# Loading the first q and k group ahead of the first W3 quarter, with new load and clock numbers in the build-time planner

## The chip, the cores and the metric

The kernel runs on one core of one Trainium2 chip. The metric is device microseconds of one execution; lower is better. The span of a profile is about 2 us shorter than the measured time of the same execution.

## The reference, cut to what matters

```python
q_n = q / (norm(q) + 1e-6);  k_n = k / (norm(k) + 1e-6)     # q, k, v: (8, 12, 448, 64)
attn = softmax(q_n @ k_n.T / tau)                            # tau = 0.1
x = (attn @ v), heads put side by side                       # (3584, 768)
a = x @ w1;  b = x @ w2                                      # 768 x 1024 each
return ((a * b) @ w3) @ w_out                                # 1024 x 1024, 1024 x 768
```

## The kernel before

The kernel multiplies W3 by W_out once, on TensorE, so that the last two products become one. It walks over 48 pairs of heads (8 batches of 6 pairs; three pairs are one load group) and fills TensorE's free time with W3 transposes, W3 x W_out products and projections. All of this is cut into small steps, and **a planner in Python decides at build time in which order each engine gets its steps**. It keeps a modelled clock for each engine and each load, and takes the step that can start first; among those within a small tolerance it takes the lowest rank. On the chip every engine runs its list in that order and waits wherever data is late. For each pair the steps are: square, sum, root and scale (they normalise q and k), a transpose on TensorE with its copy, scores, exponential, attention-times-V. The *spread* copies a loaded v group into the tile that attention-times-V reads.

```python
class Plan:
    HOP = 0.25                        # us from one engine to another
    RATE = 0.4e3                      # KB per us of the load queue
    DMA_FIRST, DMA_LAST = 1.2, 1.2
    ...
    def order(self):
        ...
        ready = {n for n, k in left.items() if k == 0}       # a set of strings
        self.lanes, ring = [], 0.0
        while ready:
            found = {}
            for n in ready:
                for eng, cost in steps[n]["on"]:
                    t = self.earliest(n, eng)
                    if t is not None:
                        found.setdefault(eng, []).append((t, n, cost))
            ...
            tmin, eng = min((min(f)[0], e) for e, f in found.items())
            tol = 0.15 if eng == "PE" else 0.05
            t, n, cost = min((f for f in found[eng] if f[0] <= tmin + tol),
                             key=lambda f: (steps[f[1]]["rank"], f[0]))
            ...
            if st["kb"]:
                ring = max(ring, t + cost + self.DMA_FIRST) + st["kb"] / self.RATE
                self.end[n], self.where[n] = ring + self.DMA_LAST, "DMA"
```

The first pair (pair 0) comes in float32 by two fast queues; all else is loaded and cast by GpSimd's queue, in this order, with at most 8 loads in flight:

```python
loads = ["w30", "q0", "k0", "wo0", "v0", "w31", "q1", "k1", "w32", "w33", "v1", "wo1", "q2",
         "k2", "w10", "v2", "w20"]        # w30: first quarter of W3; wo0: first half of W_out
...
for n in range(60):                       # warm-up on zeros: two matmuls a group, only where
    add(f"warm{n}", [("PE", 0.4)], 10000 + n, lambda e: warm(),     # nothing else can run
        takes=[("pm", ("warm", n))], later=f"warm{n - 1}" if n else None, until=11.0)
```

Of the kernel before, what the change touches and what calls it, by code (L numbers as in the profile page):

```python
# [19 lines left out]
class Plan:  # L20
# [6 lines left out]

    HOP = 0.25
    LANES = 8
    RATE = 0.4e3  # L30
    DMA_FIRST, DMA_LAST = 1.2, 1.2

    def __init__(self, rings, begin):
        self.rings, self.free = rings, dict(begin)
# [8 lines left out]
    def add(self, name, on, rank, emit, after=(), takes=(), holds=(), kb=0, later=None,  # L43
            until=None, slack=0.0, port=False):
        self.steps[name] = dict(on=on, rank=rank, emit=emit, after=list(after), later=later,
                                takes=list(takes), kb=kb, until=until, slack=slack, port=port)
        for key in holds:
            self.holders.setdefault(key, []).append(name)
# [30 lines left out]
    def order(self):  # L79
        steps = self.steps  # L80
        needs = {n: [a for a in st["after"] + [st["later"]] if a and a not in self.end]
                 for n, st in steps.items()}
        users = {}
        for n, need in needs.items():
            for a in need:
                users.setdefault(a, []).append(n)
        left = {n: len(need) for n, need in needs.items()}
        ready = {n for n, k in left.items() if k == 0}
        self.lanes, ring = [], 0.0
        self.port = dict(DVE=0.0, POOL=0.0)  # L90
        out = []
        while ready:
# [6 lines that stand above are left out]
            if not found:  # L99
                break  # L100
# [4 lines that stand above are left out]
            st = steps[n]  # L105
            out.append((t, len(out), n, eng))
            ready.discard(n)
            self.start[n], self.free[eng] = t, t + cost
            self.end[n], self.where[n] = t + cost, eng
            if st["port"] and eng in self.port:  # L110
                self.port[eng] = t + cost
# [3 lines that stand above are left out]
                self.lanes.append(self.end[n])  # L115
            for r, key in st["takes"]:
                self.taken[r].append(key)
            for u in users.get(n, ()):
                left[u] -= 1
                if left[u] == 0:  # L120
                    ready.add(u)
        late = [n for n, st in steps.items() if n not in self.end and st["until"] is None]
        assert not late, late[:10]
        return [(n, e) for _, _, n, e in sorted(out)]
# [3 lines left out]
def kernel(  # L128
# [12 lines left out]
    nc = tc.nc  # L141
# [282 lines left out]
    ident = const.tile([128, 128], BF16)  # L424

    def warm():
        ps = psM.tile([128, 512], FP32, tag="pm", name="ps_warm")
        for _ in range(2):
            nc.tensor.matmul(ps[:, :S], warm_sb[:, :128], warm_sb[:, :S], start=True, stop=True)

    def ones():
        for t in v_tiles:
            nc.gpsimd.memset(t[:, :, :, D:D + 1], 1.0)
# [5 lines left out]
        begin=dict(PE=1.0, ACT=3.0, DVE=1.2, POOL=1.3))  # L439
    add = plan.add  # L440

    add("ident", [("POOL", 0.6)], -90, lambda e: make_identity(nc, ident), later="wo0")
    add("ones", [("POOL", 0.45)], -70, lambda e: ones())
    every = slice(None)
    w3_part = [slice(k, k + 2) for k in range(0, KO2, 2)]
# [1 line left out]
                   wo0=(wo_sb, moe_w_out, every, slice(0, NH)),  # L447
                   wo1=(wo_sb, moe_w_out, every, slice(NH, DM)))
    for n, part in enumerate(w3_part):
        weights[f"w3{n}"] = (w3_sb, moe_w3, part, every)  # L450
    loads = ["w30", "q0", "k0", "wo0", "v0", "w31", "q1", "k1", "w32", "w33", "v1", "wo1", "q2",
             "k2", "w10", "v2", "w20"]
    for g in range(3, NG):
        loads += [f"q{g}", f"k{g}", f"v{g}"]
    before = None
# [157 lines left out]
                     [] if mh else [("out_sb", ("out_sb", bb, ch))], [("big", bb)],  # L613
                     holds2=[("out_sb", bb, ch)] if mh else [])
    for n in range(60):
        add(f"warm{n}", [("PE", 0.4)], 10000 + n, lambda e: warm(),
            takes=[("pm", ("warm", n))], later=f"warm{n - 1}" if n else None, until=11.0)

    for n, e in plan.order():
# [37 lines left out]
```

## Time and profile before

| | before |
|---|---|
| time, median of the first 3 runs | 406.42 us (406.42 to 406.82) |
| span of the profile | 404.3 us |
| TensorE busy | 395.0 us |
| warm-up matmuls (two in a group) | 40, 10.9 us |
| first W_out product starts | 16.50 us |
| last matmul ends | 400.17 us |

TensorE is busy almost everywhere, so the busy share says little.

### The profile page before, as it was taken

The numbers are of one execution on the slowest core, as the hardware profiler recorded it, in microseconds if no ns is written. First come the engines' busy times: TensorE is split into PE (matmuls) and PEld (weight loads), VectorE is DVE, ScalarE is ACT, GpSimd is POOL, SyncE is SP. The second block draws the span as 40 slices with busy tenths as digits, with TensorE's granted clock in tenths as the row PEclk, the third lists the DMA queues.
The fourth block names the chain that finished last, engine by engine and source line by source line (L and its number), as shares of the span: only waits on it lengthen the run. The fifth ranks groups of instructions, "written<-read, shape, count | busy, mean of one in ns | idle before, by whom it ended". The sixth has DMA issues, their size and how long they took to land.

```text
span 404.3 us, 9387 instructions
## 1 busy us (share of the span) xinstructions
PE 395.0 (98%) x3944; PEld 234.9 (58%) x3944; DVE 216.3 (53%) x484; ACT 247.9 (61%) x399; POOL 245.9 (61%) x258
## 2 busy tenths in 40 slices
PE   8799999999999999999999999999999999999995
PEld 3466665556555666555655566556655566555553
DVE  2785647587576755766655766444344443420310
ACT  3687777766676676757776757566656676323222
POOL 7479899999999999999999999315100000000000
PEclk9899999999999999999999999999999999999999
DMA  8999999256585285753745365000210013103005
GB/s 144 201 206 207 210 199 153 36 70 104 119 102 71 36 153 113 101 68 36 141 82 70 38 106 123 30 2 2 79 39 2 2 41 84 36 0 105 14 5 153
DMA packets 42474, 35.18 MB, mean 87 GB/s; under 512 B 1856, under 2 KB 36416, under 8 KB 42432
## 3 DMA queue, kind: packets, MB, share of 16 engines
q0 software_dynamic: 37312, 23.11, 41.0%
q1 hardware_dynamic: 4752, 11.07, 9.4%
q8 instruction: 31, 0.51, 0.5%
q10 hardware_dynamic: 368, 0.40, 0.3%
q14 instruction: 11, 0.09, 0.1%
HBM read 46.66 MB, written 11.01 MB: 143 GB/s over the span
## 4 chain that ended last, share of the span: by engine, by line
PE 73%; POOL 19%; DMA 3%; issue 2%; DVE 1%; ACT 0%; POOLq 0%; DVEq 0%
PE ps_b L336 15%; PE ps_a L336 14%; PE ps_o L336 14%; PE ps_av L301 10%; PE sc L284 9%; POOL sq L229 8%; POOL nrm L255 7%; PE ps_w L336 5%; PE ps_tr L268 4%; DMA wo_sb<-in_moe_w_out_dram 3%; PE ps_tb L323 2%; POOL raw L198 2%; POOL v_sb L214 2%; PE ps_w L349 1%; POOL w_sb L217 0%
## 5 line engine op out<-in xcount | busy, mean ns | idle before, releaser
L292 ACT ACTIVATE expT<-sc 112x896 bf16<-112x896 f32 x192 | 166.0, 916 | 43.2 <-PE sc L284 42.9
L336 PEld LDWEIGHTS <-w_sb 128*128 128x128 bf16 x768 | 69.6, 98 | 57.2 <-issue 4.1
L255 POOL TENSOR_TENSOR nrm<-raw,rn 112x512 bf16<-112x512 bf16 x90 | 90.8, 1036 | 2.2 <-PE ps_tr L268 2.1
L229 POOL TENSOR_TENSOR sq<-raw 112x512 bf16<-112x512 bf16 x87 | 87.8, 1037 | 0.2
L336 PE MATMUL ps_b<-xT,w_sb 128*128 128x448 bf16 x384 | 83.2, 353 | 0.0
L336 PE MATMUL ps_a<-xT,w_sb 128*128 128x448 bf16 x384 | 83.0, 352 | 0.0
L336 PE MATMUL ps_o<-w_sb,abT 128*128 128x384 bf16 x448 | 80.1, 326 | 0.0
L235 DVE TENSOR_REDUCE ss<-sq 112x8 f32<-112x512 bf16 x96 | 64.0, 679 | 15.2 <-POOL sq L229 14.9
L382 DVE TENSOR_TENSOR abT<-a_sb,ps_b 128x448 bf16<-128x448 bf16 x64 | 39.6, 619 | 57.7 <-PE ps_b L336 54.8
L301 PEld LDWEIGHTS <-expT 112*128 112x128 bf16 x1536 | 59.2, 98 | 19.4 <-issue 8.8
L371 ACT CAST a_sb<-ps_a 128x448 bf16<-128x448 f32 x64 | 34.0, 532 | 52.4 <-PE ps_a L336 51.5
L301 PE MATMUL ps_av<-v_sb,expT 112*128 112x65 bf16 x1536 | 65.2, 194 | 0.0
L284 PE MATMUL sc<-qkT 64*112 64x448 bf16 x384 | 56.9, 374 | 1.4 <-DVE qkT L276 1.3
L336 PEld LDWEIGHTS <-abT 128*128 128x128 bf16 x448 | 41.3, 98 | 26.5 <-issue 2.7
L342 ACT COPY out_sb<-ps_o 128x384 f32<-128x384 f32 x43 | 20.6, 478 | 38.0 <-PE ps_o L336 36.5
L314 DVE TENSOR_TENSOR osd<-ps_av,rs 128x256 bf16<-128x256 f32 x96 | 40.7, 424 | 3.3
L313 DVE RECIPROCAL rs<-ps_av 128x4 f32<-128x4 f32 x96 | 17.1, 178 | 46.2 <-PE ps_av L301 45.9
L214 POOL COPY v_sb<-vraw 112x1536 bf16<-112x1536 bf16 x16 | 23.4, 1460 | 24.4 <-PE ps_av L301 24.0
L276 DVE COPY qkT<-ps_tr 128x896 bf16<-128x896 bf16 x48 | 29.7, 619 | 12.1 <-PE ps_tr L268 12.1
L330 DVE COPY xT<-ps_tb 128x448 bf16<-128x448 bf16 x48 | 18.6, 387 | 20.5 <-PE ps_tb L323 20.2
L284 PEld LDWEIGHTS <-qkT 64*112 64x112 bf16 x384 | 17.3, 125 | 20.7 <-issue 16.4
L268 PEld LDWEIGHTS <-nrm 112*128 112x128 bf16 x384 | 21.9, 99 | 12.1 <-issue 6.6
(37 smaller groups left out, 220.3 us busy)
## 6 DMA issues: line engine op xcount, KB each, us to landing
vraw<-in_v_dram POOLq DMA_DIRECT2D x16, 336.0 KB, 4.8
raw<-in_q_dram POOLq DMA_DIRECT2D x15, 336.0 KB, 5.6
raw<-in_k_dram POOLq DMA_DIRECT2D x15, 336.0 KB, 7.6
w_sb<-in_moe_w_dram POOLq DMA_DIRECT2D x2, 1536.0 KB, 25.4
out_dram<-out_sb SPq DMA_DIRECT2D x7, 336.0 KB, 2.8
out_dram<-out_sb SPq DMA_DIRECT2D x8, 288.0 KB, 3.0
w_sb<-in_moe_w_dram POOLq DMA_DIRECT2D x4, 512.0 KB, 16.2
out_dram<-out_sb SPq DMA_DIRECT2D x8, 240.0 KB, 2.8
```

The lines of the kernel that those rows point to most:

```text
L214: nc.gpsimd.tensor_copy(v_tiles[g % NV][:, :, :, :D], vraws.pop(g))
L229: eng.tensor_mul(o, x, x)
L235: nc.vector.reduce_sum(sss[g][:, t, 2 * i:2 * i + 2, :], sqs.pop((g, i, t)), axis=AX.X)
L255: eng.tensor_mul(nrms[g][:, i, t].rearrange("p j h d -> p h j d"), raw_of(g, t, i), rns[g][:, t, 2 * i:2 * i + 2].to_broadcast([P, 2, NJ, D]))
L268: nc.tensor.transpose(ps[:, t, j * P:(j + 1) * P], n[:, i, t, j].rearrange("p h d -> p (h d)"), ident[:P, :P])
L284: nc.tensor.matmul(sc[:P, hh, :S], qks[pp][64 * hh:64 * hh + 64, 1, c * P:(c + 1) * P], qks[pp][64 * hh:64 * hh + 64, 0, :], start=True, s ...
L292: nc.scalar.activation(exps[pp][:, c], scs.pop((pp, c))[:P, :, :S], ACT.Exp, scale=1.0 / float(tau))
L301: nc.tensor.matmul(ps[:, m, :], exps[pp][:, c, hh, q0:q0 + 128], vt[:, 2 * i + hh, c, :], start=(c == 0), stop=(c == NJ - 1))
L314: nc.vector.tensor_mul(osds[pp][:, :, hh, :], ps[:, :, :D], rs.to_broadcast([128, NJ, D]))
L336: nc.tensor.matmul(o, l, r, start=(i == 0), stop=(i == len(pairs) - 1))
L371: nc.scalar.copy(a_sbs[b, fo], pms.pop(("a", b, fo))[:, :S])
L382: nc.vector.tensor_mul(abts[b // 2][:, fo, c0:c0 + S], a_sbs.pop((b, fo)), pms.pop(("b", b, fo))[:, :S])
```

## The change

The intent: the first q and k group land sooner so that attention can start, and the planner is told what the load queue and the cold TensorE clock really take, so that its order fits. The diff is complete.

```diff
--- before.py
+++ after.py
@@ -27,8 +27,9 @@
 
     HOP = 0.25
     LANES = 8
-    RATE = 0.4e3
-    DMA_FIRST, DMA_LAST = 1.2, 1.2
+    RATE = 0.385e3
+    RING_FREE = 3.8
+    DMA_FIRST, DMA_LAST = 1.2, 1.5
 
     def __init__(self, rings, begin):
         self.rings, self.free = rings, dict(begin)
@@ -86,7 +87,7 @@
                 users.setdefault(a, []).append(n)
         left = {n: len(need) for n, need in needs.items()}
         ready = {n for n, k in left.items() if k == 0}
-        self.lanes, ring = [], 0.0
+        self.lanes, ring = [], self.RING_FREE
         self.port = dict(DVE=0.0, POOL=0.0)
         out = []
         while ready:
@@ -439,7 +440,7 @@
         begin=dict(PE=1.0, ACT=3.0, DVE=1.2, POOL=1.3))
     add = plan.add
 
-    add("ident", [("POOL", 0.6)], -90, lambda e: make_identity(nc, ident), later="wo0")
+    add("ident", [("POOL", 0.6)], -90, lambda e: make_identity(nc, ident), later="w30")
     add("ones", [("POOL", 0.45)], -70, lambda e: ones())
     every = slice(None)
     w3_part = [slice(k, k + 2) for k in range(0, KO2, 2)]
@@ -448,8 +449,8 @@
                    wo1=(wo_sb, moe_w_out, every, slice(NH, DM)))
     for n, part in enumerate(w3_part):
         weights[f"w3{n}"] = (w3_sb, moe_w3, part, every)
-    loads = ["w30", "q0", "k0", "wo0", "v0", "w31", "q1", "k1", "w32", "w33", "v1", "wo1", "q2",
-             "k2", "w10", "v2", "w20"]
+    loads = ["q0", "k0", "w30", "wo0", "v0", "w31", "q1", "k1", "w32",
+             "w33", "v1", "wo1", "q2", "k2", "w10", "v2", "w20"]
     for g in range(3, NG):
         loads += [f"q{g}", f"k{g}", f"v{g}"]
     before = None
@@ -613,7 +614,7 @@
                      [] if mh else [("out_sb", ("out_sb", bb, ch))], [("big", bb)],
                      holds2=[("out_sb", bb, ch)] if mh else [])
     for n in range(60):
-        add(f"warm{n}", [("PE", 0.4)], 10000 + n, lambda e: warm(),
+        add(f"warm{n}", [("PE", 0.78 if n < 4 else 0.39)], 10000 + n, lambda e: warm(),
             takes=[("pm", ("warm", n))], later=f"warm{n - 1}" if n else None, until=11.0)
 
     for n, e in plan.order():
```

## The prediction

> **What bounds the kernel now.** I read the page first, then the chain of waits in order of time, then the timeline of the first 30 us, then windows of 1 us over the first 24 us. The page says where time can be lost at all:
>
> ```profile
> PE 395.0 (98%) x3944; PEld 234.9 (58%) x3944; DVE 216.3 (53%) x484; ACT 247.9 (61%) x399; POOL 245.9 (61%) x258
> ```
>
> TensorE is idle for 404.3 - 395.0 = 9.3 us of the span. The timeline places it: 1.26 us before the first warm-up matmul, 404.3 - 400.17 = 4.1 us after the last matmul (last copy and store), some 2.6 us between 11 and 17 us, and about 1.2 us in all the rest (windows: 0.78 us lost between 100 and 177 us, 0.37 between 177 and 300, nothing after). So from 16.5 us on TensorE is a queue of work, and the end is 16.5 + that work + 4.1. The other engines have slack (61% at most); the long stretch of GpSimd in the chain from 95 to 177 us ends in a TensorE wait of only 0.37 us. A change of load order can pay only in what TensorE does before that queue starts, in its clock there, and in new holes. Busy there isn't useful: 32 + 8 matmuls of the head are warm-up on zeros, 10.9 us.
>
> ```profile
> 3.58 12.87 DMA wo_sb<-in_moe_w_out_dram
> 16.50 2.02 PE ps_w L336 x8
> ```
>
> The chain of waits: the first half of W_out is issued at 3.58 us and lands 12.9 us later; from its landing the chain is TensorE. Its wait itself is short (0.73 us). What had TensorE done by then that is useful?
>
> ```profile
> 4.45 0.63 ACT L227 ACTIVATE sq<-raw 112x512 bf16<-112x512 f32 x1 [1.96 <-DMA raw<-in_k_dram]
> 10.17 1.06 PE L349 MATMUL ps_w<-ident,w_sb 128*128 128x128 bf16 x16
> 10.82 1.29 DVE L344 COPY w3t_sb<-ps_w 128x1024 bf16<-128x1024 bf16 x2 [3.32 <-PE ps_w L349]
> 11.28 0.63 ACT L227 ACTIVATE sq<-raw 112x512 bf16<-112x512 bf16 x1 [3.50 <-DMA raw<-in_q_dram]
> 12.02 0.68 DVE L235 TENSOR_REDUCE ss<-sq 112x8 f32<-112x512 bf16 x1
> 12.62 0.68 DVE L255 TENSOR_TENSOR nrm<-raw,rn 112x512 bf16<-112x512 f32 x1
> 13.29 0.56 PE L268 MATMUL ps_tr<-ident,nrm 112*128 112x112 bf16 x8
> 15.19 0.59 PE L284 MATMUL sc<-qkT 64*112 64x448 bf16 x4 [1.34 <-DVE qkT L276]
> 16.81 0.90 ACT L292 ACTIVATE expT<-sc 112x896 bf16<-112x896 f32 x1
> ```
>
> The key reading is the sixth line. Pair 0 comes by its own fast queues at 4.2 to 4.5 us, and ScalarE has its last root (rn, 7.57 + 0.21 us) at 7.8. Its second scale could run then; it runs at 12.62, because VectorE takes its instructions in program order and the planner put before it the two W3 copies (10.82, W3 landed about 9.5) and the sum of a square that waits for the q group (landed 11.3). The planner had thought these loads earlier: with its numbers (0.4 MB/us, ring free at 0, 1.2 + 1.2 us) W3 lands at 3.3 + 2.62 + 1.2 = 7.1, q0 at 8.3, W_out at 13.3. Landed: 9.5, 11.3, 16.5. Useful TensorE work before 16.5 us is thus two W3 transposes, one pair transpose, half the scores of pair 0, at warm durations about 1.06 + 0.45 + 0.55 = 2.1 us. The holes have a price too:
>
> ```profile
> 14.00:15.00 1.00, 0.00 (x0) 0.00 (x0) 1.00 (x3) 0.94 (x4) 0.15 (x2) 1.00 1.43 201
> 17.00:18.00 1.00, 1.00 (x6) 0.53 (x5) 1.00 (x2) 0.71 (x1) 0.62 (x1) 0.65 1.21 199
> 18.00:19.00 1.00, 1.00 (x10) 0.83 (x8) 0.23 (x1) 0.46 (x2) 0.47 (x1) 0.50 1.37 202
> 19.00:20.00 1.00, 0.91 (x7) 0.38 (x5) 0.62 (x1) 1.00 (x3) 1.00 (x2) 0.50 1.38 197
> 20.00:21.00 1.00, 1.00 (x11) 0.61 (x11) 0.00 (x0) 1.00 (x2) 0.79 (x2) 0.64 1.44 199
> ```
>
> The last three columns are granted clock, DMA share, GB/s. TensorE stands still at 14 to 15 us and is then given half its clock: missing clock 0.35 + 0.50 + 0.50 + 0.36 = 1.7 us.
>
> **What the Trainium skill says.** "TensorE: Matmul & The Clock Gate", Part 1, says the clock is half speed by default, that about 3.4 us of sustained work releases it, and that an idle window of the same free-running length takes it back. The trace agrees in kind: the warm-up's weight loads come every 0.37 us up to 7.1 and every 0.19 us after, and the slow spell above lasts from 17.35 to about 20.7 = 3.4 us. "DMA: Bandwidth & Descriptors", Anatomy of one DMA, puts a load through GpSimd at about 2.0 us plus bytes over 436 GB/s. Steady flow agrees: W_out (1.57 MB read) lands 16.5 - 12.7 = 3.8 us after k0, 0.41 MB/us. The first 10 us don't: they move 138 to 172 GB/s of written bf16 a microsecond, against about 200 later.
>
> **The change, part by part.** No arithmetic is added or removed; all instructions keep their costs. Three things move.
>
> (1) q0 and k0 (0.46 MB read each) go ahead of the first W3 quarter (1.05 MB). Landings are my estimate: the same bytes through the same queue. From about 4.4 us at the measured 0.15 MB/us written: q0 is 0.23 MB written, 1.5 us, and about 1.3 us to completion: 7.3; k0 8.8; W3 comes last of the three and takes k0's old place, 12.3 to 12.7. The sum of the three is unchanged, so W_out stays at 16.5, v0 18.5, the second W3 quarter about 20.9, q1 22.5, k1 24.7, the third quarter 27.0. Gain for q0 and k0 about 4 us, loss for W3 about 3.
>
> (2) The planner's new numbers, worked by hand: q0 3.8 + 1.19 + 1.5 = 6.5, k0 7.7, W3 10.4, W_out 14.5, v0 16.3, second quarter 19.0, third 25.3. Against my real landings they are still early by about 2 us, no longer by 3. Pair 0's second scale is planned at about 8.4 and the W3 copies only after 11, so the scale goes ahead of them.
>
> (3) Warm-up: four groups at 0.78, the rest at 0.39. The planner fills TensorE to about 9.5 with some 18 groups in place of 16. In the trace 8 groups are slow (16 matmuls in 5.9 us), so it is still too many: 1.26 + 8 x 0.735 + 10 x 0.375 = 10.9 us. That, and no longer the data, should gate pair 0's transposes.
>
> Then, with the durations above: transposes at 10.9 (13.29 before); copy to 12.1; the W3 transposes, planned ahead of the first scores, at 12.5 when W3 has landed; first scores about 13.0 (15.19 before); first exponential about 13.2 (16.81). By W_out's landing TensorE can have done both W3 transposes, two pair transposes, all scores of pair 0: 1.06 + 2 x 0.45 + 2 x 0.55 = 3.1 us, 1.0 more than before. If TensorE then isn't idle long enough to lose its clock, another 1.5 us: 2.5 us. Against that stands v0: it still lands at 18.5, and its spread (1.48 us on GpSimd) gives 20.1 at best, 20.8 as traced before. Before, the first attention-times-V came at 22.7, late enough; now TensorE will have W_out products (2 x 1.3), the scores of pair 1 and a transpose, all done near 20.0, and wait some 0.8 us. Net 2.5 - 0.8 = 1.7 us. A second count agrees: the work done by 22.54 before (a third W3 transpose instead of a second half of scores, both about 0.5 us) is done by 20.85. After that TensorE is a queue again and the lead should last to the end: 406.42 - 1.7 = 404.7.
>
> **Rivals.** (a) The head stays bound by loads: W_out, v0 and the weight quarters keep their times, and TensorE meets each as late as before, above all the third quarter at 27.0, where it waited 0.43 us already. For it: the before order tracks the planner at a constant lag of 3 us there (13.55 planned, 16.5 run; 23.95 and 27.0). Against it: q1 and k1 leave plenty of attention work in reserve at that time. It would make 406. (b) GpSimd becomes the bound: it is over 90% busy from 30 to 250 us, and its stream starts with q1, which doesn't come sooner. For it: the chain goes through it for 80 us. Against it: TensorE lost only 0.78 us in that stretch, as the projections fill whatever attention leaves. It would eat the whole gain: 406.4. (c) Everything fits: the clock stays up, no wait for v0, the two stray holes vanish: 406.42 - 4 = 402.4. (d) The new order, fixed at build time, meets new holes of 0.5 to 1 us, or the slow clock comes one window later because W3 is late: 407.5. One more spread: ties of the planner are settled by the order of a set of strings, which needn't be the same in two builds, so a few tenths either way are order luck.
>
> **Range and chances.** The middle is 404.7; (a) and (b) pull up by 1.7, (c) down by 2.3. I give 402.2 to 407.0 eight in ten. Two per cent is 8.1 us; the whole head has only 2.6 us of idle time, 1.7 of lost clock and 10.9 of warm-up that mostly waits for data, so faster by 2% is nearly ruled out, as is slower.
>
> **What would show it.** Right: pair 0's transposes at about 11 us after more warm-up matmuls (36 or so in a row), first q-group square near 7.5, W3 transposes near 12.5, W_out products still at 16.5, no window of half clock between 17 and 21, first attention-times-V near 21, a last matmul 1.7 us sooner. Wrong: W_out's landing moved by over 1 us, half clock again, or TensorE busy time from 30 us on lower by over 1 us.

## The result

In the same rounds the changed kernel took 405.87 us (median of 4 runs, 404.98 to 406.30) and the kernel before 406.42. Ratios here are the mean time of one kernel's runs over that of the other's of the same rounds, so not quite the ratio of the medians. It is 0.9983, with a 95% interval of 0.9964 to 1.0003. In microseconds that is -0.7 (+0.1 to -1.5). The forecast of -1.7 lies outside.

TensorE's row of the page of the changed kernel, to be held against 395.0:

```profile
PE 392.7 (97%) x3944; PEld 233.5 (58%) x3944; DVE 217.9 (54%) x487; ACT 246.0 (61%) x396; POOL 245.9 (61%) x258
```

TensorE is busy 2.3 us less, but the span is only 0.4 us shorter: more of it is now idle. The timeline of the changed kernel (start, length, engine, line, what; in brackets the idle time before and what ended it) answers to the one of before:

```profile
7.09 0.63 ACT L228 ACTIVATE sq<-raw 112x512 bf16<-112x512 bf16 x1 [0.33 <-DMA raw<-in_q_dram]
8.75 0.69 DVE L256 TENSOR_TENSOR nrm<-raw,rn 112x512 bf16<-112x512 f32 x1 [0.32 <-ACT rn L251]
10.03 0.56 PE L269 MATMUL ps_tr<-ident,nrm 112*128 112x112 bf16 x8
10.81 1.06 PE L350 MATMUL ps_w<-ident,w_sb 128*128 128x128 bf16 x16
11.80 0.58 PE L285 MATMUL sc<-qkT 64*112 64x448 bf16 x4
12.82 1.73 ACT L293 ACTIVATE expT<-sc 112x896 bf16<-112x896 f32 x2
13.40 0.37 PE L269 MATMUL ps_tr<-ident,nrm 112*128 112x112 bf16 x4 [1.01 <-DVE nrm L256]
14.95 1.46 PE L337 MATMUL ps_w<-wo_sb,w3t_sb 128*128 128x384 bf16 x8
19.27 0.67 PE L302 MATMUL ps_av<-v_sb,expT 112*128 112x65 bf16 x16 [1.13 <-POOL v_sb L215]
```

The q group is squared at 7.1 instead of 11.3. Pair 0's second scale runs at 8.75 as soon as its root is there, ahead of the W3 copies (12.62 before). Pair 0 is transposed at 10.0 instead of 13.3, and the first exponential starts at 12.8 instead of 16.8. The first attention-times-V comes 3.4 us sooner and does wait for v0's spread, 1.1 us. Windows of 1 us of the changed kernel (from the left: stretch and length, then busy time of TensorE, its weight loads, VectorE, ScalarE and GpSimd; the last three columns are the granted clock as a share of full speed, DMA share, GB/s):

```profile
17.00:18.00 1.00, 0.76 (x10) 0.56 (x10) 0.37 (x1) 1.00 (x3) 1.00 (x2) 1.00 1.16 194
18.00:19.00 1.00, 0.13 (x3) 0.02 (x1) 0.63 (x1) 0.80 (x1) 1.00 (x1) 1.00 1.42 205
19.00:20.00 1.00, 0.73 (x21) 0.73 (x21) 0.03 (x1) 0.00 (x0) 0.80 (x2) 1.00 1.45 189
```

There are holes, but the clock stays at 1.00 where it was 0.50 before. So the head went about as foretold. To see where its lead went I count, from the matmuls that the trace lists, the useful work done by a given time: each group at the length that the chain of waits shows when it runs back to back at full clock (W_out and output products 1.30 us for 8, projections 1.14 for 6, attention-times-V 0.62 for 16, scores 0.52 for 4, pair transposes 0.40 for 8, back transposes 0.22 for 4, W3 transposes 0.46 for 8, warm-up nothing). By 38 us the kernel before had started 56 W_out products, 64 W3 transposes, 28 scores, 32 pair transposes, 64 attention-times-V matmuls and 8 back transposes, worth 20.9 us; the changed kernel 54, 64, 32, 40, 96 and 12, worth 23.0. Time less useful work is **lost time**, which includes idle time, warm-up and slow clock: 17.1 and 15.0 us at 38 us. The useful work of a whole execution is the same 381.9 us in all of them, so lost time at the last matmul decides. (With the lengths rounded as printed here the sum is 382.4; then all lost times at the last matmul are 0.5 us smaller, and no difference between kernels moves.)

| lost time, us, by | 16 us | 38 us | 60 us | last matmul |
|---|---|---|---|---|
| before | 14.2 | 17.1 | 16.9 | 18.3 |
| changed | 12.1 | 15.0 | 16.3 | 17.8 |
| lead of the change | 2.1 | 2.1 | 0.7 | 0.5 |

The lead of 2 us was won and kept for 38 us, and 1.4 us of it was given back in the next 22. Windows from 38 to 100 us, first before, then changed:

```profile
38.00:100.00 62.00, 62.00 (x710) 37.97 (x709) 41.66 (x96) 43.76 (x68) 58.60 (x60) 1.00 0.88 131
```

```profile
38.00:100.00 62.00, 60.97 (x670) 36.67 (x669) 39.32 (x89) 42.02 (x67) 56.92 (x59) 1.00 0.85 124
```

TensorE is busy for every one of the 62.00 us in the kernel before, and idle for 1.03 us in the changed one. The chain of waits of the changed kernel names half of it (that the count says 1.4 us and not 1.03 may come from counting whole matmuls by their start; this isn't shown):

```profile
36.24 1.05 POOL nrm L256
37.29 0.99 POOL sq L230
38.28 1.00 POOL nrm L256
39.28 0.05 issue
39.33 0.37 PE ps_tr L269 x4
```

A transpose waits 0.55 us for a scale on GpSimd, in whose list a square stands ahead of it. This is the picture of the prediction's rival (b), once. At 60.15 another transpose waits 0.48 us until VectorE has emptied the one PSUM buffer for transposes (a copy to xT). The two waits together are the 1.03 us. These are holes of an order that fits the chip badly by tenths of a microsecond. Does such a hole belong to the change, or does any order have its own?

### The profile page after: what moved, and what is told of

Read it like the earlier page. It is cut to its first block, busy times and chain, and to the rows that moved or that the text cites. A ratio compares the mean times of both kernels' runs of the same rounds, so it can differ in the third digit from the quotient of the medians.

```text
span 403.9 us, 9389 instructions
## 1 busy us (share of the span) xinstructions
PE 392.7 (97%) x3944; PEld 233.5 (58%) x3944; DVE 217.9 (54%) x487; ACT 246.0 (61%) x396; POOL 245.9 (61%) x258
## 4 chain that ended last, share of the span: by engine, by line
PE 80%; POOL 12%; DMA 4%; issue 2%; DVE 1%; ACT 0%; POOLq 0%
PE ps_b L337 17%; PE ps_a L337 17%; PE ps_o L337 16%; PE ps_av L302 11%; PE sc L285 10%; POOL nrm L256 4%; PE ps_tr L269 4%; DMA raw<-in_k_dram 4%; POOL sq L230 3%; PE ps_w L337 3%; PE ps_tb L324 3%; POOL raw L199 1%; POOL v_sb L215 1%; POOL vraw L206 1%; POOL w_sb L218 1%
## 5 line engine op out<-in xcount | busy, mean ns | idle before, releaser
L343 ACT COPY out_sb<-ps_o 128x384 f32<-128x384 f32 x39 | 18.7, 478 | 39.3 <-PE ps_o L337 37.6
L269 PE MATMUL ps_tr<-ident,nrm 112*128 112x112 bf16 x384 | 27.3, 213 | 2.7 <-DVE nrm L256 1.2
L285 PEld LDWEIGHTS <-qkT 64*112 64x112 bf16 x384 | 17.4, 125 | 20.9 <-issue 17.6
```

The costliest lines, as they stand in the source:

```text
L269: nc.tensor.transpose(ps[:, t, j * P:(j + 1) * P], n[:, i, t, j].rearrange("p h d -> p (h d)"), ident[:P, :P])
L285: nc.tensor.matmul(sc[:P, hh, :S], qks[pp][64 * hh:64 * hh + 64, 1, c * P:(c + 1) * P], qks[pp][64 * hh:64 * hh + 64, 0, :], start=True, s ...
```

## The experiments

**What a build draws.** The planner walks over a Python set of strings, so equal candidates are taken in the order of the set, which differs from one Python process to the next. Two builds of the same unchanged text have different instruction lists. So I gave the ties a fixed rule. Theory: the change wins about 2 us in the head and loses most of it later. Rival: the difference measured is luck of the ties.

Rule a takes equal candidates by name, rule b by a checksum of the name, rule c in the order in which the steps were added:

```diff
-            for n in ready:
+            for n in sorted(ready):                                                      # rule a
+            for n in sorted(ready, key=lambda x: zlib.crc32((x + 'b').encode())):        # rule b
+            for n in sorted(ready, key=place.get):    # rule c; place = {n: i for i, n in enumerate(steps)}
```

> The kernel before with the planner's ties settled by name, so that every build gives the same program. Theory (the new loads win about 2 us in the head and lose most of it after 38 us on the q and k preparation): within 0.4 us of the kernel before, 406.0 to 406.8. Rival (the measured 0.5 us is luck of the tie order): 0.5 us or more away from it.

> The changed kernel with ties by name. Theory: 405.4 to 406.3, and 0.3 to 0.8 us below the tied kernel before; the useful work of TensorE leads by 1.5 to 2.5 us at 30 us and by less than 1 us at 60. Rival (luck of ties): the difference to the tied kernel before has another sign or size than 0.5.

> The kernel before with the ties settled by a hash of the name instead. Theory: within 0.4 us of the same with ties by name. Rival: they differ by as much as the change does (0.5 us or more).

> The changed kernel with the ties settled by the same hash. Theory: again 0.3 to 0.8 us below the kernel before of the same ties. Rival: it differs from the changed kernel with ties by name by 0.5 us or more, and the lead at 60 us scatters.

> The kernel before, ties settled by the order in which the steps were added (third rule). Theory (luck of the tie order is several us, the change is worth about 2 us on top of it): anywhere from 404 to 412.

> The changed kernel with the third rule. Theory: 1 to 3 us below the kernel before of the same rule, as with rules a (1.9) and b (3.0). Rival (the change is worth nothing, both gaps were luck): the gap has the other sign or is under 0.5.

| rule | before, us | ratio | changed, us | ratio | gap of the ratios |
|---|---|---|---|---|---|
| a | 412.19 | 1.0158 | 410.30 | 1.0107 | -0.51% (-2.1 us) |
| b | 410.38 | 1.0091 | 407.42 | 1.0022 | -0.69% (-2.8 us) |
| c | 411.60 | 1.0134 | 409.08 | 1.0066 | -0.68% (-2.8 us) |

The ratios are to the first kernel before in the same rounds, which took 406.1 to 406.7. For rules a and b my expectations failed in size; for c, written after them, they held. The rule of ties alone moves the same kernel by 1.5 to 6 us, far more than my 0.4. But the change wins 2 to 3 us under each rule; the 95% intervals of the two ratios lie apart for b and c and just overlap for a. The lost time of the traces says where the orders differ: from 38 us to the end it grows by 4.8 to 6.3 us in the three tied kernels before and by 1.7 to 5.7 in the changed ones, against 1.2 and 2.8 in the first pair. That the gain is won in the head is not shown under the rules: by 38 us the changed kernel leads by 0.8 us (a) and 1.1 us (c) and is 3.4 us behind under b, where its trace holds a stretch of half clock and the other doesn't. Each trace is one execution; the execution times of these six are 0.7, 2.0 and -0.25 us apart, the medians 1.9, 2.5 and 3.0 (in the order a, c, b). All three rules make slower kernels than the drawn orders; why is not settled.

**The same texts, built once more.** Only a comment is added at the end, here of the first two:

```diff
+# built once more
```

Theory: the first build of before was an unusually good draw. Rival: it was the same program each time, or the new ones are bad draws.

> The kernel before, word for word, built once more. If ties were all that the first builds differed by and each build draws them anew: another order of TensorE's instructions than in the first trace, and a time up to 3 us away from 406.1, with as wide a gap as between the tied orders a and b (1.8 us). If the build is the same program each time: the same order, and 406.1 within 0.4.

> The changed kernel, word for word, built once more. Ties drawn anew: another order, up to 3 us away from 405.9. Same program: the same order and 405.9 within 0.4.

> Another fresh build of the kernel before, word for word. Theory (the first build of before was a good draw): 407.5 to 411, its lost time growing by over 1.5 us from 38 us to the end. Rival (408.3 was a bad draw): 406.0 to 407.0.

> Another fresh build of the changed kernel. Theory (the change is worth 2 to 3 us over builds): 404.5 to 408, on average 405.5 to 406.5 over the four builds. Rival (405.1 was a good draw, the change is worth half a microsecond): as slow as the builds of before, 406 to 409.

> Another fresh build of the kernel before. Theory: 407.5 to 411. Rival: 406.0 to 407.0.

> Another fresh build of the changed kernel. Theory: 404.5 to 408. Rival: 406 to 409.

| build | time, us | ratio | lost by 16 us | by 38 us | by last matmul |
|---|---|---|---|---|---|
| before, first | 406.42 | 1 | 14.2 | 17.1 | 18.3 |
| before_again | 408.32 | 1.0046 | 13.7 | 18.0 | 19.9 |
| before_again2 | 407.34 | 1.0025 | 14.2 | 16.2 | 19.1 |
| before_again3 | 407.60 | 1.0032 | 12.9 | 17.4 | 19.2 |
| changed, first | 405.87 | 0.9983 | 12.1 | 15.0 | 17.8 |
| after_again | 405.12 | 0.9971 | 12.9 | 14.5 | 16.7 |
| after_again2 | 405.28 | 0.9975 | 12.3 | 13.9 | 16.2 |
| after_again3 | 406.48 | 1.0010 | 12.3 | 17.7 | 19.7 |

The lists of matmuls of the first two builds of before differ from the 55th matmul on, in 2248 of 3944 places; those of the changed kernel from the 133rd on. Another order makes other waits. Who waited for whom on TensorE, longest first (us in total, times, longest), in the first build and in before_again:

```profile
PE sc L284 <- DVE qkT L276: 1.3, 1, 1.3
PE ps_warm L429 <- DVE warm_sb L423: 1.3, 1, 1.3
PE ps_w L336 <- DMA wo_sb<-in_moe_w_out_dram: 0.7, 1, 0.7
```

```profile
PE ps_av L301 <- POOL v_sb L214: 1.8, 1, 1.8
PE ps_warm L429 <- DVE warm_sb L423: 1.3, 1, 1.3
PE sc L284 <- DVE qkT L276: 1.1, 2, 0.6
```

The wait of 1.8 us for v0's spread, which I had expected from the change, comes in a build of the old text. All three new builds of before are slower than the first, one of them (407.34) a little less than the 407.5 that I had set as the lower end. The changed builds lie at 405.1 to 406.5.

The mean ratio of the four builds is 1.0026 before and 0.9985 changed: a gap of -0.41%, or -1.7 us. With the scatter of four builds each (standard deviation 0.19% and 0.18%) the 95% interval is about -0.1 to -0.7%. The mean lead in lost time is 1.3 us at 16 us, 1.9 us at 38 us and 1.5 us at the last matmul. So over builds the lead of the head mostly lasts. Part of it is chance: all four traces of before hold a stretch of half clock, and one of the four of the changed kernel. The first pair joined the fastest build of before to a middling one of the changed kernel, and their growth after 38 us is the smallest (1.2) of the builds of before and the largest (2.8) of the changed ones. The runs beside which everything was measured have medians of 406.1 to 406.7 in five sets of rounds, so I take that they are one build, the first; this is inferred.

**Which part does it: the loads or the plan?** Under rule c the order of every engine can be held still while two loads swap places on GpSimd. loads_only_c is the kernel before with only q0 and k0 issued ahead of W3; plan_only_c is the changed kernel with only W3 issued ahead again:

```diff
-    for n, e in plan.order():
+    line_up = plan.order()
+    moved = [x for x in line_up if x[0] in ('q0', 'k0')]          # plan_only_c: ('w30',)
+    line_up = [x for x in line_up if x not in moved]
+    at = [x[0] for x in line_up].index('w30')                     # plan_only_c: 'q0'
+    for n, e in line_up[:at] + moved + line_up[at:]:
```

> Third tie rule, the kernel before with its own planned order on TensorE, VectorE and ScalarE unchanged; only GpSimd issues q0 and k0 ahead of the first W3 quarter. Theory (the gain lies in the planned order, not in the landings): no gain, or up to 1 us slower than the kernel before of this rule, as the W3 transposes, planned first, now wait until about 11. Rival (the landings are the gain): 1 to 2.5 us faster.

> Third tie rule, the changed kernel with its own planned order; only GpSimd issues the first W3 quarter ahead of q0 and k0 again. Theory: pair 0 is transposed as early as in the changed kernel (about 10 to 11 us), pair 1 comes 2 to 3 us later, 0 to 1.5 us slower than the changed kernel and still 1 us or more below the kernel before of this rule. Rival (the landings are the gain): as slow as the kernel before, 411.6.

loads_only_c took 412.40 us (ratio 1.0138 against 1.0134): no gain, as the theory said. Timeline of the kernel before under rule c, then with the loads alone:

```profile
9.59 1.06 PE L350 MATMUL ps_w<-ident,w_sb 128*128 128x128 bf16 x16
12.33 0.56 PE L269 MATMUL ps_tr<-ident,nrm 112*128 112x112 bf16 x8
```

```profile
10.52 1.07 PE L350 MATMUL ps_w<-ident,w_sb 128*128 128x128 bf16 x16 [0.81 <-DMA w_sb<-in_moe_w_dram]
13.28 0.56 PE L269 MATMUL ps_tr<-ident,nrm 112*128 112x112 bf16 x8
```

The q group lands at 6.5, but TensorE's and VectorE's lists still put W3 first, and W3 is later by the swap: pair 0 is transposed 0.95 us later than before. plan_only_c took 410.12 us (ratio 1.0084): the plan alone wins 0.50% (2.0 us; the 95% intervals lie apart). The loads seem to add 0.18% (0.7 us) once the plan is there, but this is not clear of noise (1.0063 to 1.0105 and 1.0052 to 1.0080). Nor is it shown that the 2.0 us are won in the head: by 38 us the trace of plan_only_c has lost 16.8 us, before_tie_c 16.1. New numbers in the planner make a new order of everything, so that this one order is also better further on remains possible. My detail for it was wrong. Half of pair 0's transposes ran at 10.25, the other half only at 13.02:

```profile
12.27 0.69 DVE L257 TENSOR_TENSOR nrm<-raw,rn 112x512 bf16<-112x512 f32 x1 [0.32 <-ACT rn L252]
13.02 0.37 PE L270 MATMUL ps_tr<-ident,nrm 112*128 112x112 bf16 x4 [2.41 <-DVE nrm L257]
```

ScalarE's list under this rule has the square of the q group ahead of pair 0's second root, so pair 0 waits for a load that it doesn't need. It is the fault of the kernel before, now on another engine.

**The slow clock.** In some executions TensorE runs 3 us or more of the head at half clock. The changed kernel under rule b, an execution with a granted mean of 0.996:

```profile
20.00:21.00 1.00, 0.78 (x14) 0.78 (x15) 0.43 (x2) 0.00 (x0) 0.54 (x1) 0.67 1.43 199
21.00:22.00 1.00, 1.00 (x17) 1.00 (x15) 0.71 (x3) 0.00 (x0) 0.44 (x1) 0.50 1.24 217
22.00:23.00 1.00, 1.00 (x7) 0.66 (x6) 0.25 (x1) 0.54 (x1) 0.39 (x1) 0.50 1.12 208
```

The same program had a granted mean of 0.993 to 0.996 in four executions, which took 407.1 to 408.0 us, and 1.000 in two, which took 405.6 and 405.8: about 2 us. In the first build of before it costs less: of its 40 later executions 20 had a mean of 0.996 or less and took 406.63 us on average, the other 20 took 406.25. The mean alone doesn't place the stretch: in the trace of loads_only_c it lies at 251 us. A mean of 0.996 or less came in 31 of 54 executions of the four builds of before (the runs beside counted as the first build), and in 6 of 18 of the changed ones, 4 of these 6 in after_again3. To see whether holes in the head cause it, I let warm-up matmuls fill planned gaps up to 20 us:

```diff
-            takes=[("pm", ("warm", n))], later=f"warm{n - 1}" if n else None, until=11.0)
+            takes=[("pm", ("warm", n))], later=f"warm{n - 1}" if n else None, until=20.0)
```

> Third tie rule, the changed kernel with warm-up matmuls allowed in planned gaps up to 20 us in place of 11 (5 more groups of two). Theory (a slow-clock window of 3.4 us in some executions costs about 1.7 us): no execution with a granted mean under 0.998, against one of six; the median within 0.6 us of the changed kernel of this rule (409.1), the spread narrower. Rival (the clock comes from the phase of the window alone): the share of slow executions stays.

> Tie rule b (a hash of the name), the changed kernel with warm-up matmuls allowed in planned gaps up to 20 us. With rule b and 11 us, 4 of 6 executions had a granted mean of 0.993 to 0.996 and took 407.1 to 408.0, the two with 1.0 took 405.6 and 405.8. Theory (holes cause the slow stretch, it costs about 2 us): no execution under 0.998, all within 405.3 to 406.6. Rival (chance): again about half slow, median above 407.

> The changed kernel's own text, ties drawn at build, warm-up to 20 us. Theory: no execution under 0.998; 404.5 to 406, no worse than the four builds of the changed kernel on average (405.7). Rival: executions under 0.997 as before, 405 to 407.

| | executions at 0.996 or less | time, us | ratio |
|---|---|---|---|
| rule c, until 11 | 1 of 6 | 409.08 | 1.0066 |
| rule c, until 20 | 0 of 6 | 409.09 | 1.0068 |
| rule b, until 11 | 4 of 6 | 407.42 | 1.0022 |
| rule b, until 20 | 2 of 6 | 406.98 | 1.0020 |
| drawn ties, until 20 | 0 of 6 | 405.43 | 0.9961 |

Under rule b two executions were still slow (408.9 and 409.5 us), so filling planned gaps isn't enough, and the expectation of none fell. The count fell from 11 slow ones of 30 (the first four builds and rules b and c) to 2 of 18, which speaks for the holes, but the edit also adds steps and draws other ties. It remains open how much is cause and how much is chance. The last row beats the first build of before clear of noise (0.9947 to 0.9975), as after_again does (0.9949 to 0.9992). It has the lowest ratio of all, but against the 0.9971 of after_again it is a tie. Drawn ties don't give that program again.

**A wider margin in the planner.** If the late holes come from hand-overs that take longer than planned, doubling the planned one should remove them:

```diff
-    HOP = 0.25
+    HOP = 0.5
```

> Third tie rule, the changed kernel with the planner's time from engine to engine doubled to 0.5 us, so that it places an instruction later behind what it needs. Theory (after the head, TensorE loses 5.7 us with this rule at waits on copies and sums that come a few tenths later than planned): at least 1.5 us faster than 409.1, the growth of lost time from 38 us to the end falling from 5.7 to under 4. Rival (those losses are unavoidable, or order luck that any reshuffle draws anew): anywhere between 404 and 412 with the growth unchanged on average.

It took 419.28 us (1.0316), 10 us slower. Windows from 38 to 100 us of the changed kernel under rule c, then with the wide margin:

```profile
38.00:100.00 62.00, 60.55 (x648) 37.01 (x645) 40.75 (x90) 39.59 (x65) 56.91 (x59) 1.00 0.89 131
```

```profile
38.00:100.00 62.00, 57.75 (x613) 34.62 (x612) 37.55 (x84) 39.72 (x66) 58.77 (x60) 0.97 0.88 128
```

TensorE is idle 4.25 us in this stretch in place of 1.45. The theory fell: with the margin this order fits the chip worse, not better. It is again a new order, and one draw of it. What in it did the harm I haven't traced.

## Why the prediction was wrong

**The bound** was read rightly: the useful work is the same in every trace, and the end moves with what TensorE loses around it.

**Landings and order in the head.** q0 at 7.1 (7.3 foretold), k0 at 8.2 (8.8). W3 landed at 10.8 (12.3 to 12.7), and W_out at 14.9, not unmoved at 16.5; a move of over 1 us was one of the prediction's signs of being wrong. The prediction's rate for the first 10 us, 138 to 172 GB/s, holds from 4 us on only: its own windows have 198 and 296 between 2 and 4 us. In the traces of the other six kernels with the old text's loads W_out landed between 13.0 and 16.1, in the other six of the changed one between 14.5 and 15.3, so the first trace of before was late by chance as well. Pair 0 was transposed at 10.0 (10.9). The number of warm-up matmuls was right, 38 in a row (some 36 foretold), but the clock was released at about 4.5 us, not at 7.1 (from there weight loads come every 0.19 us and no longer every 0.37; the clock column has no record of the time before and reads 1.00 there). The wait for v0 was 1.1 us (0.8). The sum, 1.7 us, was 2.1 in the first pair and 1.9 on average over builds.

**The step that failed** is "After that TensorE is a queue again and the lead should last to the end: 406.42 - 1.7 = 404.7", together with the term "so a few tenths either way are order luck". TensorE isn't a queue with one fixed amount of lost time behind the head. Each built order has holes of its own, worth 1.2 to 2.9 us in the eight drawn builds and up to 6.3 us under the fixed rules. A build moves the time by up to 1.9 us for one and the same text (406.4 to 408.3). The order luck that I set at tenths was as large as the effect. The sign that the prediction named for this, TensorE's busy time from 30 us on lower by over 1 us, is there (367.3 us against 369.0), but it tells nothing: work done before 30 us lowers it too, and after_again2, which kept its lead, has 366.2. What tells is TensorE's idle time from 30 us to the last matmul: 2.5 us against 1.2. The first pair met the best build of before, and 1.6 us of the lead of 2.1 went into the difference of later holes. Over the four builds of each text lost time grows after 38 us by 2.0 us before and by 2.3 changed, so most of those 1.6 us belong to the two draws.

**A term that was mis-sized** is "another 1.5 us" for the clock. It was read off one trace with the slow stretch. In the first build of before half of the executions go without it and are only 0.4 us faster (95% interval about -0.1 to 0.8). So within one program, too, an advantage of 1.7 us in the head seems to be mostly gone at the end. Where it goes, and what else differs between these executions, no trace shows.

Over four builds of each text the gap is -1.7 us (about -0.4 to -3). It agrees with the forecast, but that the numbers are equal is luck: the interval is wide, and the gap hardly comes from the clock. Executions without the slow stretch (a mean over 0.996) average 406.8 us over the four builds of before and 405.2 over the three of the changed kernel that have any (three of the builds of before have one each).

**The rivals.** (a) fell: the changed kernel met the loads with a lead that lasted past 27 us. (b) happened once, at 39 us, for 0.55 us; the three other builds of the changed kernel don't list a wait of TensorE for a scale on GpSimd, so it isn't a bound. (c) fell: there was a wait for v0, and the holes did not vanish. (d) came closest, but its cause is mostly the draw and not the new loads. The slow stretch was absent in all four executions of the first changed kernel, but that is a matter of chance: 6 of 18 executions of the changed builds have it.

## What to carry to other kernels

When an order is planned at build time and ties are left to a set, two builds of the same text are two different kernels: fix the ties or build several times before believing a difference of half a per cent. Count useful work done by a given time and not busy time, and a lead that was won and lost again can be seen in a trace. A cost that one trace shows, as the 1.7 us of slow clock, has to be compared over many executions before it is counted as a gain. Under rule c, loads that land sooner were worth nothing with lists that weren't planned for them.

## What the Trainium skill lacked or had wrong

- "TensorE: Matmul & The Clock Gate", Part 1, has the slow clock come back after an idle window. In the first trace of before it came back at 17.3 us although the windows show TensorE busy for about 1.4 of the 3.4 us ahead of it; the page doesn't say how much work is enough to keep the clock.
- The same section says of the ramp at the start that its penalty is run-variable and under 1% of a typical span. The later slow stretch is of that size here too: about 2 us of 406 in one program (0.5%), in 4 of its 6 executions, and 0.4 us on average in the first build of before. That is the size of the effects that are sought in a tuned kernel.
- "DMA: Bandwidth & Descriptors", Anatomy of one DMA, has no figure for the first load of a queue. By its formula 1.05 MB and 0.46 MB take an estimated 4.4 and 3.1 us; as the first load they took 5.6 to 8.5 us (W3 in the traces of before, drawn and tied) and 5.3 to 6.3 us (q0 in the changed ones). In all of these the two fast loads of pair 0 and the next loads of the queue were in flight beside them, so it is not the formula's case of one DMA.
- No page has a word on orders that a build draws anew; they moved this kernel by 0.5% among drawn builds and by up to 1.6% under fixed rules.
